# Two PSUM banks that change roles at the end of each group of heads

## The chip, the cores and the metric

The kernel runs on one core of one Trainium2 chip. The metric is the device time of one execution in microseconds (us); the time given for a kernel is the median of its runs.

## The reference, cut to what matters

Four layers are stacked on a residual stream `x` of 2048 tokens by 576 features: attention (A), linear attention (B), A, B. All the work that the change touches lies in the two A layers and in that part of the B layers that is done while A still runs.

```
def _A_ref(x, wq, wk, wv, wo):                      # 32 heads of 18, one shared k and v
    q = (x @ wq).reshape(B, S, H, Dh).transpose(0, 2, 1, 3)
    k, v = x @ wk, x @ wv
    scores = einsum("bhqd,bkd->bhqk", q, k) * Dh ** -0.5
    p = softmax(scores)
    return einsum("bhqk,bkd->bhqd", p, v).transpose(...).reshape(B, S, H * Dh) @ wo

x = x + _A_ref(_layernorm(x), A_wq, A_wk, A_wv, A_wo)
x = x + _B_ref(_layernorm(x), B_wqkv, B_w_phi, B_wo)   # feature maps, per-head state, read-out
x = x + _A_ref(...)
x = x + _B_ref(...)
```

## The kernel before

**Tiling of the attention.** The 2048 queries are four chunks of 512 (`CW`), the 32 heads eight groups of four (`NG`, `GH`). A layer thus has 32 pairs of chunk and group, the list `groups`; below, "group" means such a pair. For each group the program runs over the 16 key tiles `t` of 128 keys. For one key tile it makes the scores of four heads (four matmuls, line 451, into two tiles `sc` of two heads each), takes their exponentials on ScalarE (line 952, `pt<-sc`), and multiplies them into the sum (`add_values`, line 738: four matmuls of 32 rows, one for each head, into the tile `acc`). The sum over the 16 key tiles builds up in `acc`, one PSUM bank of 128 x 512 floats. In the trace each of the matmuls of line 738 has two records, so one key tile shows as x8; in the order of the program's instructions it shows as x4.

**PSUM.** There are eight banks. While `attend` runs, three tiles `sc` take six of them, `acc` one (pool `psa`, one buffer) and `ps` one (pool `psm`, one buffer). Through `ps` goes everything that is not attention.

**Units, bursts and the fill.** `attend` cuts the work of groups 1 to 31 into units of one key tile and two heads. It issues three units of scores (a burst), then sums, then three more units, and so on; the sums run behind the scores. After every second burst it calls `fill()`, which takes one step of other work from a queue called `bulk`: the folding of the feature weights (`fold_phi`, lines 290 to 321; first layer only), and then, for each finished chunk, its output projection and most of the B layer (`chunk_work`: projections at line 205, `update_state` at line 526). A step writes one tile `ps`, and a copy or an addition on VectorE reads it. A projection is 14 matmuls; its cost on the program's own scale is 1750, over `HEAVY`, and then the sum of that burst is put off: the next one takes three key tiles. Smaller steps are followed at once by the sum of one key tile. So TensorE's order repeats every six units: six score matmuls, a step of fill, its sums, six score matmuls, its sums. This is called a period below. `in_order` chains TensorE's instructions in the order in which they are written.

**The end of a group.** After the sixteenth key tile, `finish_group` copies `acc` to SBUF on VectorE (line 865, `osb<-acc`), and sends the denominators through DRAM and back (lines 867 to 883). The next group's sum goes to a new tile `acc` of the same pool. The pool has one buffer, so the first matmul of the next group waits until the copy at line 865 has ended. TensorE executes in order: score matmuls and fill behind the waiting matmul wait too. Where the group ends inside a burst, the first matmuls of the next group stand right behind the last ones of this group; where it ends with the burst, six score matmuls, and perhaps a step of fill, stand between them.

For what follows the 30 ends of groups that matter in a layer are numbered: boundary k lies between the sums of groups k and k + 1, with k from 1 to 30.

## Time and profile before

| | |
|---|---|
| time, median of 3 runs | 2824.49 us (2821.88 to 2828.26) |
| the profiled execution: its time, its span | 2827.11 us, 2825.3 us |
| attention of the first layer, `attend` | about 168 to 1243 us of the span |
| attention of the second layer | about 1560 to 2632 us |
| TensorE busy, over the span | 2658.9 us (94%) |
| ScalarE busy | 2189.0 us (77%) |
| VectorE busy | 1242.3 us (44%) |

The page of the profile adds up busy times over the span. A wait has a row of its own in the view of waits: who waited, for whom, the total, how often, and the longest. In the timeline every row gives the start, the length, the engine, the line, what is written and read, how many instructions were merged (x8), and in brackets how long the engine stood idle ahead of it and for what. "PE" is TensorE's matmuls, "PEld" its weight loads, "DVE" VectorE, "ACT" ScalarE, "SPq" the queue that issues the DMAs. The end of a matmul is modelled: matmuls overlap, so that the matmuls of one key tile start 0.11 us apart and each is shown with some 0.59 us.

### The profile page before, as it was taken

To read this page: it belongs to the slowest core of one execution; us is meant where nothing else is said; L and a number is where in the kernel's file an instruction comes from. 1 tells how busy PE (TensorE), PEld (TensorE's weight loads), DVE (VectorE), ACT (ScalarE), POOL (GpSimd) and SP (SyncE) were. 2 spreads that over 40 slices of the span, in tenths; PEclk is the share of its full clock that TensorE was granted. 3 is DMA by queue.
4 is the path that set the end of the run, shared out by engine and by line. 5 is a ranking of instruction groups with operands and counts; after the bars stand their busy time and mean duration, and the time that the engine had idled before them with its cause. 6 is when DMAs were issued, how large, how long until landed. Compare 5 with 4: busy or idle time off the path is not lost. (4 is left out here: it accounts for less than half of the span.)

```text
span 2825.3 us, 55543 instructions
## 1 busy us (share of the span) xinstructions
PE 2658.9 (94%) x22094; PEld 1458.3 (52%) x22094; DVE 1242.3 (44%) x2899; ACT 2189.0 (77%) x2644; POOL 86.0 (3%) x123
## 2 busy tenths in 40 slices
PE   6989999998999899998999888999989998999989
PEld 5733335443454345468986222355435453455788
DVE  6421224542355334558763301145424542454675
ACT  4579998898889888964345899989888888898521
POOL 1000000000000000004000000000000000000110
PEclk9999999999999999999999999999999999999999
DMA  5322233222222223234632311132123212321344
GB/s 184 103 67 62 67 97 92 61 48 57 71 81 54 58 58 96 52 80 120 186 123 89 87 37 34 43 94 60 42 65 99 57 39 68 91 62 43 103 119 139
DMA packets 355814, 224.97 MB, mean 80 GB/s; under 512 B 206874, under 2 KB 288986, under 8 KB 355546
## 3 DMA queue, kind: packets, MB, share of 16 engines
q1 hardware_dynamic: 355546, 221.31, 28.3%
q8 instruction: 178, 2.92, 0.4%
q14 instruction: 90, 0.74, 0.1%
HBM read 132.88 MB, written 67.03 MB: 71 GB/s over the span
## 5 line engine op out<-in xcount | busy, mean ns | idle before, releaser
L952 ACT ACTIVATE pt<-sc 128x1024 f32<-128x1024 f32 x1984 | 1874.5, 1031 | 216.3 <-PE sc L451 197.5
L738 PE MATMUL acc<-pt,vst 128*32 128x512 f32 x7936 | 966.6, 604 | 33.0 <-DVE osb L865 33.0
L451 PE MATMUL sc<-qst,kst 56*128 56x512 f32 x3840 | 696.3, 448 | 63.7 <-ACT pt L952 63.2
L451 PEld LDWEIGHTS sc<-qst,kst 56*128 56x128 f32 x3840 | 320.9, 185 | 620.8 <-ACT pt L952 556.0
L738 PEld LDWEIGHTS acc<-pt,vst 128*32 128x32 f32 x7936 | 209.5, 110 | 470.0 <-issue 401.0
L205 PE MATMUL ps<-wahi,xs 128*128 128x288 f32 x1035 | 226.5, 305 | 1.0 <-ACT xs L137 0.9
L205 PEld LDWEIGHTS ps<-wahi,xs 128*128 128x128 f32 x1035 | 170.0, 189 | 18.9 <-issue 12.7
L865 DVE COPY osb<-acc 128x512 f32<-128x512 f32 x62 | 42.6, 688 | 295.5 <-PE acc L738 266.2
L205 PE MATMUL ps<-walo,xs 128*128 128x288 f32 x575 | 169.3, 296 | 0.0
L262 DVE TENSOR_TENSOR xc<-xc,ps 128x288 f32<-128x288 f32 x77 | 34.5, 449 | 217.9 <-PE ps L205 217.9
L205 PE MATMUL ps<-wchi,on 128*128 128x288 f32 x549 | 121.7, 306 | 1.8 <-DMA on<-parts 1.8
L205 PE MATMUL ps<-wchi,xs 128*128 128x288 f32 x540 | 119.7, 307 | 1.7 <-ACT wchi L137 1.6
L205 PE MATMUL ps<-wbhi,xs 128*128 128x288 f32 x540 | 118.5, 305 | 0.0
L229 POOL TENSOR_TENSOR rstd<-var,neghalf 128x1 f32<-128x1 f32 (+1 forms) x56 | 33.1, 592 | 2534.5 <-DVE var L227 1755.1
L205 PEld LDWEIGHTS ps<-walo,xs 128*128 128x128 f32 x575 | 108.7, 189 | 0.0
L883 DVE TENSOR_TENSOR osb<-osb,parts 128x512 f32<-128x512 f32 x62 | 42.6, 688 | 139.7 <-DMA parts<-den_rows 139.7
L355 PE MATMUL ps<-xsc,wbhi 128*128 128x256 f32 x513 | 98.3, 287 | 5.8 <-DVE xsc L140 2.3
L205 PEld LDWEIGHTS ps<-wchi,on 128*128 128x128 f32 x549 | 90.2, 188 | 19.2 <-issue 16.6
L205 PEld LDWEIGHTS ps<-wchi,xs 128*128 128x128 f32 x540 | 88.4, 188 | 20.0 <-issue 17.5
L205 PEld LDWEIGHTS ps<-wbhi,xs 128*128 128x128 f32 x540 | 88.3, 188 | 17.5 <-issue 15.7
L137 ACT ACTIVATE xs<-ps 128x512 fp32r<-128x512 f32 x34 | 20.3, 596 | 93.3 <-PE ps L248 93.2
L205 PE MATMUL ps<-wclo,xs 128*128 128x288 f32 x300 | 89.0, 297 | 2.3 <-DVE wclo L140 2.3
(282 smaller groups left out, 2944.0 us busy)
## 6 DMA issues: line engine op xcount, KB each, us to landing
qst<-qd SPq DMA_DIRECT2D x360, 72.0 KB
pht<-phi SPq DMA_DIRECT2D x32, 540.0 KB
qd<-pcs SPq DMA_DIRECT2D x64, 256.0 KB
parts<-den_rows SPq DMA_DIRECT2D x62, 256.0 KB
wstage<-folded SPq DMA_DIRECT2D x50, 288.0 KB
on<-parts SPq DMA_DIRECT2D x192, 72.0 KB
phi<-pht SPq DMA_DIRECT2D x96, 144.0 KB
wstage<-in_A_wo_dram SPq DMA_DIRECT2D x32, 288.0 KB
```

The lines of the kernel that those rows point to most:

```text
L137: A.activation(dst_hi, src, AF.Copy)
L205: T.matmul(dst, xs[:, slot, :], w[half][:, k, c0 : c0 + HALF], start=(n == 0), stop=(n == last))
L229: G.tensor_tensor(rstd, var, neghalf[:, :n], op=ALU.pow)
L262: V.tensor_add(xr, xr, po)
L355: T.matmul(po, lhs, xsc[:, slot, :], start=(n == 0), stop=(n == LASTP))
L451: T.matmul(sc, kst[head_rows(h), t * P : (t + 1) * P], q[head_rows(h), h // 2, :], start=True, stop=True)
L738: T.matmul(acc[32 * j : 32 * j + 32, :], vst[:, t, :], pts[j], start=first, stop=last)
L865: V.tensor_copy(osb, acc[c, g])
L883: V.tensor_mul(osb, osb, den)
L952: A.activation(pt, sc, AF.Exp, scale=SCALE)
```

## The change

The banks `acc` and `ps` trade their roles. `homes` holds the two places; a new sum takes the first, and every tile of the fill takes the second (`Spare`). At the first sum of a group the list is reversed, except for group 1, whose place is the usual one. The last group of a layer has the usual place again, since 30 reversals lie between. A small function `bank` cuts a tile of the wanted shape out of a bank. The loop of bursts is written as two functions, `scores` and `sums`; the rest is the same work.

```diff
+            homes = [(psa, "acc"), (psm, "ps")]
+
+            class Spare:
+                def tile(self, shape, dtype, name):
+                    return bank(*homes[1], shape)
...
-                    bulk.append(after_chunk(c, on[c], psm, loads))
+                    bulk.append(after_chunk(c, on[c], Spare(), loads))
...
             def values(c, g, t, pt):
                 if t == 0:
-                    acc[c, g] = psa.tile([P, CW], F32, name="acc")
+                    if (c, g) != groups[1]:
+                        homes.reverse()
+                    acc[c, g] = bank(*homes[0], [P, CW])
...
-            bulk.append(extra(a1, psm, loads))
+            bulk.append(extra(a1, Spare(), loads))
...
-                    pt = a1.tile([P, 2, 512], F32, name="pt", bufs=9)
+                    pt = a1.tile([P, 2, 512], F32, name="pt", bufs=3 * BURST)
...
+            while at[0] < len(units):
+                sums(scores(BURST))
                 tick()
-                if not odd:
-                    tick()
-            for n, t, _ in units[2 * done :: 2]:
-                values(*groups[n], t, [pts.pop((n, t, hh)) for hh in range(2)])
                 tick()
+                ready = scores(BURST)
+                spent = fill()
                 in_order()
+                if spent < HEAVY:
+                    sums(ready)
+                tick()
...
+    def bank(pool, tag, shape):
+        t = pool.tile([P, CW], F32, name=tag)[: shape[0]]
+        if len(shape) == 2:
+            return t[:, : shape[1]]
+        return t[:, : shape[1] * shape[2]].rearrange("p (a b) -> p a b", b=shape[2])
```

The instructions of TensorE and of ScalarE stand in the same order as before; on TensorE only the bank that each writes is another. The places on which the prediction rests are these.

TensorE at boundary 8 of a layer (`wchi`, `wclo` are the output projection's weights, `on` the normalised sums), before:

```order
L205 MATMUL ps<-wclo_2485,on 128x288
L451 MATMUL sc<-qst,kst 128x512 x6
L738 MATMUL acc<-pt,vst 32x512 x12
L451 MATMUL sc<-qst,kst 128x512 x6
L205 MATMUL ps<-wchi,on 128x288
```

and now:

```order
L205 MATMUL acc<-wclo_2485,on 128x288
L451 MATMUL sc<-qst,kst 128x512 x6
L738 MATMUL ps<-pt,vst 32x512 x8
L738 MATMUL acc<-pt,vst 32x512 x4
L451 MATMUL sc<-qst,kst 128x512 x6
L205 MATMUL ps<-wchi,on 128x288
```

The twelve matmuls are two key tiles of the old group and one of the new. Before, all wrote one bank; now the third key tile writes the bank that the projection ahead of it used, and the projection behind it takes the bank that the copy of the old group reads.

TensorE at boundary 3 of the first layer, where a step of `fold_phi` (line 312) stands right ahead of the new group's first key tile, before:

```order
L738 MATMUL acc<-pt,vst 32x512 x8
L451 MATMUL sc<-qst,kst 128x512 x6
L312 MATMUL ps<-featq,xn 128x126 x4
L738 MATMUL acc<-pt,vst 32x512 x4
L451 MATMUL sc<-qst,kst 128x512 x6
```

and now:

```order
L738 MATMUL acc<-pt,vst 32x512 x8
L451 MATMUL sc<-qst,kst 128x512 x6
L312 MATMUL ps<-featq,xn 128x126 x4
L738 MATMUL ps<-pt,vst 32x512 x4
L451 MATMUL sc<-qst,kst 128x512 x6
```

The step of fill and the first sum of the new group now write the same bank, one right behind the other.

VectorE's queue is ordered by a scheduler, and some instructions trade places with their neighbours. The copy of a group's sum moves behind other work at boundary 7 of the first layer (a pair of weight instructions) and at boundaries 15 and 23 of both; at boundary 15 it stood so (`wstage`, `wchi`, `wclo` are the output projection's weights on their way in):

```order
L576 STREAM_TRANSPOSE pht<-featq 128x1152
L865 COPY osb<-acc 128x512
L139 CAST wchi<-wstage 128x576
L140 TENSOR_TENSOR wclo_7440<-wstage,wchi 128x576
L873 RECIPROCAL rd<-rd 128x16
```

and now stands so:

```order
L576 STREAM_TRANSPOSE pht<-featq 128x1152
L140 TENSOR_TENSOR wclo_7440<-wstage,wchi 128x576
L139 CAST wchi<-wstage 128x576
L140 TENSOR_TENSOR wclo_7440<-wstage,wchi 128x576
L870 COPY osb<-acc 128x512
L878 RECIPROCAL rd<-rd 128x16
```

The splitting of two pieces of weights has moved ahead of the copy. At boundary 10, of which the prediction also speaks, VectorE's order is the same before and now.

## The prediction

> **What bounds the kernel now.** The page comes first, for the bound and for the group that the change touches.

> ```profile
> span 2825.3 us, 55543 instructions
> PE 2658.9 (94%) x22094; PEld 1458.3 (52%) x22094; DVE 1242.3 (44%) x2899; ACT 2189.0 (77%) x2644; POOL 86.0 (3%) x123
> ...
> L738 PE MATMUL acc<-pt,vst 128*32 128x512 f32 x7936 | 966.6, 604 | 33.0 <-DVE osb L865 33.0
> ...
> L865 DVE COPY osb<-acc 128x512 f32<-128x512 f32 x62 | 42.6, 688 | 295.5 <-PE acc L738 266.2
> ```

> TensorE is busy for 94% of the span. Ahead of the sums (line 738) it idles 33.0 us, all of it for the copy of a group's sum, which takes 0.69 us. The view of waits for TensorE says how often.

> ```profile
> PE sc L451 <- ACT pt L952: 67.9, 200, 1.8
> PE acc L738 <- DVE osb L865: 33.0, 34, 2.4
> ...
> PE ps L205 <- DVE wclo L140: 2.3, 5, 0.9
> ...
> PE ps L205 <- DMA on<-parts: 1.8, 2, 0.9
> ```

> There are 34 waits, in 62 copies. The boundaries without one have six score matmuls or a fill between the old group's last sum and the new group's first. Whether a wait costs time is a question for the stage, since 67.9 us of waits for ScalarE show that TensorE is not the bound everywhere. So I read the timeline in a stretch with projections (boundary 26, second layer):

> ```profile
> 2454.55 2.78 PE L738 MATMUL acc<-pt,vst 128*32 128x512 f32 x24
> ...
> 2461.20 1.92 PE L738 MATMUL acc<-pt,vst 128*32 128x512 f32 x16
> ...
> 2463.20 0.69 DVE L865 COPY osb<-acc 128x512 f32<-128x512 f32 x1 [2.41 <-PE acc L738]
> ...
> 2463.94 1.07 PE L738 MATMUL acc<-pt,vst 128*32 128x512 f32 x8 [0.81 <-DVE osb L865]
> ...
> 2468.88 2.78 PE L738 MATMUL acc<-pt,vst 128*32 128x512 f32 x24
> ```

> From the sums of one period to the next it is 2461.20 - 2454.55 = 6.65 us; the period with the boundary takes 2468.88 - 2461.20 = 7.68. It is longer by 1.03, not by 0.81: the ends of matmuls are modelled, and without a wait a key tile starts while the one ahead still counts as running. (Three key tiles take 2.78, one 1.07, so they start 0.86 apart; the third would have started at 2461.20 + 1.72 = 2462.92, and started 1.02 later.) I take **0.2 us on top of the wait that the profile shows**.

> In the second layer's first stretch there is no fill, and ScalarE should be the bound:

> ```profile
> 1621.48 1.92 PE L738 MATMUL acc<-pt,vst 128*32 128x512 f32 x16
> ...
> 1627.28 1.06 PE L738 MATMUL acc<-pt,vst 128*32 128x512 f32 x8
> 1629.16 1.07 PE L738 MATMUL acc<-pt,vst 128*32 128x512 f32 x8 [0.81 <-DVE osb L865]
> ...
> 1634.10 1.92 PE L738 MATMUL acc<-pt,vst 128*32 128x512 f32 x16
> ...
> 1630.76 2.85 ACT L952 ACTIVATE pt<-sc 128x1024 f32<-128x1024 f32 x3 [1.22 <-PE sc L451]
> ```

> A period there is 1627.28 - 1621.48 = 5.80, with the boundary 1634.10 - 1627.28 = 6.82: again 1.02 more. ScalarE ran dry for 1.22 us, because the next scores stand behind the waiting sum. So the wait is paid in both kinds of stretch.

> **The change part by part.** *The 34 waits go.* The new group writes another bank. Two of the 34 (boundary 28 of each layer) have score matmuls between, so nothing overlapped there and the 0.2 is not added: 33.0 + 32 x 0.2 = 39.4 us.

> *Two of them cost more than the wait.* At boundary 25 of each layer the copy stands behind a transposition in VectorE's queue:

> ```profile
> 749.68 1.06 PE L738 MATMUL acc<-pt,vst 128*32 128x512 f32 x8 [1.50 <-DVE osb L865]
> ...
> 1036.61 0.65 DVE L865 COPY osb<-acc 128x512 f32<-128x512 f32 x1
> 1037.32 3.44 PE L738 MATMUL acc<-pt,vst 128*32 128x512 f32 x16 [2.37 <-DVE osb L865]
> 1041.71 0.40 PE L205 MATMUL ps<-wchi,on 128*128 128x288 f32 x1
> ...
> 2427.44 3.28 PE L738 MATMUL acc<-pt,vst 128*32 128x512 f32 x16 [2.35 <-DVE osb L865]
> ...
> 1037.30:1040.70 3.40, 3.38 (x18) 0.60 (x18) 0.00 (x0) 0.00 (x0) 0.00 (x0) 0.54 0.40 69
> 749.70:750.70 1.00, 1.00 (x10) 0.16 (x10) 0.00 (x0) 0.00 (x0) 0.00 (x0) 1.00 0.00 0
> ```

> After waits of 2.37 and 2.35 us two key tiles take 3.44 and 3.28 instead of 1.92, and the granted clock in that stretch (the column ahead of the DMA share) is 0.54. After the next longest wait, 1.50 us at boundary 17, it is 1.00. Without the wait the slow matmuls go too: 1.52 + 1.36 = 2.9 us more. [...]

> *One wait comes back.* At boundary 10 of each layer VectorE splits weights behind the copy:

> ```profile
> 498.82 0.69 DVE L865 COPY osb<-acc 128x512 f32<-128x512 f32 x1 [1.56 <-PE acc L738]
> ...
> 503.71 0.46 DVE L139 CAST wchi<-wstage 128x576 fp32r<-128x576 f32 x1 [1.87 <-DMA wstage<-folded]
> ...
> 504.20 0.76 DVE L140 TENSOR_TENSOR wclo<-wstage,wchi 128x576 fp32r<-128x576 f32 x1
> ...
> 505.02 0.40 PE L205 MATMUL ps<-wclo,xs 128*128 128x288 f32 x1 [0.39 <-DVE wclo L140]
> ```

> This chain starts when the old group's last sum ends, which the change doesn't move, and goes over a DMA; TensorE already waits for its end at 505.02. It would come 1.0 earlier and wait 1.0 longer: **-2.0 us** in two layers.

> *Two new waits.* At boundaries 3 and 6 of the first layer a step of fill writes the bank right ahead of the new group:

> ```profile
> 268.81 1.06 PE L738 MATMUL acc<-pt,vst 128*32 128x512 f32 x8
> 268.92 0.68 DVE L314 COPY featk<-ps 128x504 f32<-128x504 f32 x1 [1.30 <-PE ps L312]
> 363.28 1.06 PE L738 MATMUL acc<-pt,vst 128*32 128x512 f32 x8
> 363.39 0.28 DVE L296 COPY xn<-ps 72x128 f32<-72x128 f32 x1 [0.40 <-PE ps L295]
> ```

> The sum must wait for the end of the copy, from 268.81 to 269.60 and from 363.28 to 363.67, and 0.05 for the signal: 0.85 + 0.45 = **-1.3 us**. Behind them wait the next scores, and ScalarE for these.

> *No cost I expect at the other boundaries,* for two covers. First, where a projection stands ahead, six score matmuls stand between it and the new sum. The tightest kind (14 boundaries, k = 9, 12 and the like):

> ```profile
> 570.91 0.29 PE L205 MATMUL ps<-walo,xs 128*128 128x288 f32 x1
> ...
> 571.24 0.46 DVE L482 COPY featk<-ps 128x288 f32<-128x288 f32 x1 [2.25 <-PE ps L205]
> ...
> 572.10 1.49 PE L738 MATMUL acc<-pt,vst 128*32 128x512 f32 x11
> ```

> The bank is read out at 571.70, 0.40 before it is wanted, and VectorE had idled 2.25 before. Were that cover gone by half a microsecond, 14 x 0.5 = 7 us. Second, the next projection now writes the bank of the old sum, behind the copy. At boundary 25 it would start 4.1 earlier (2.37 + 0.2 + 1.52) than 1041.71, at 1037.6; the copy ends at 1037.26. That cover is thin, but only the boundaries with a late copy have so little. The weights that VectorE now splits ahead of the copy at boundaries 7, 15 and 23 delay a copy that nobody on TensorE waits for any more; I cost that at nothing. Instructions are neither added nor removed on TensorE and ScalarE.

> Sum: 39.4 + 2.9 - 2.0 - 1.3 = **39.0 us** less.

> **The rivals.** *Half comes back.* Scores, fill and sums are one order on TensorE, so what arrives 1.0 us earlier may meet a chain of VectorE and DMA, as at boundary 10: the finish of a group, the flipped tokens, the weights. For it speaks that this is seen once in each layer; against it, that the projections (line 205) wait for nothing else for more than the 2.3 and 1.8 us in the list above. With half of the 39.0 gone, 2824.5 - 19.5 = 2805.

> *No gain.* If TensorE only trades one wait for the next, everything comes back at the following scores, which wait for ScalarE (67.9 us of such waits): 2824. Against it stands ScalarE's 1.22 of idle time above, which the boundary made. [...]

> *Slower.* The 14 boundaries that have no wait now would get one, if VectorE read the projection's bank late: behind a feature chain or a transposition. From 2.4 us on, the slow clock adds 1.5, so that each costs 4: 14 x 4 = 56, less 39, gives 2824.5 + 17 = 2842. The point of balance is 39 / 14 = 2.8 us for each. Against it: the read-out above starts right at the projection's end, on an idle VectorE.

> **How the numbers follow.** The profiled execution took 2827.1 us with a span of 2825.3; the median of the runs is 2824.5, inside their spread of 2821.9 to 2828.3. I take the saving from the median: 2824.5 - 39.0 = 2785.5, rounded to 2786. Chances: the sum as worked out 75%, half comes back 17%, no gain 4%, slower 4%. If nothing came back (39.4 + 2.9 = 42.3) and the run were as fast as the lowest shown (2.6 below), 2779.6; if the 14 tight places lost 0.5 each (7 us) and the run were as slow as the highest (3.8 above), 2796; a little of the second case takes it to 2800. So 2779 to 2800. 0.2% (5.6 us) is about what a measurement of this kernel can tell from no change: faster 92%, same 4%, slower 4%.

> **What would show it.** In the changed profile the row of line 738 waiting for the copy of `osb` should be gone, or down to about 1.3 us with two waits, on the copies of `fold_phi`. Periods with a boundary should take 6.65 and 5.80 us. The period with boundary 10 should not get shorter, and wait longer for `wclo`. No sum should run at a slow clock behind boundary 25. The prediction is wrong if line 738 waits for other VectorE instructions in many places, if projections wait for the copy of `osb`, or if ScalarE's busy share does not rise.

## The result, and the profile after

| | before | after |
|---|---|---|
| time, median | 2827.2 us (2821.9 to 2832.3, 6 runs) | 2775.1 us (2774.5 to 2778.9, 6 runs) |
| span of the profiled execution | 2825.3 us | 2773.3 us |

The ratio is 0.9817, with a 95% interval of 0.9803 to 0.9831. The kernel got 52 us faster; the prediction said 39 and had 2779 as its lower end. The direction and the mechanism came out as forecast, but 13 us came from somewhere else. The page of the changed kernel first (busy times, then the two groups of line 738, one for each bank):

```profile
span 2773.3 us, 55536 instructions
PE 2646.9 (95%) x22094; PEld 1459.3 (53%) x22094; DVE 1243.3 (45%) x2899; ACT 2190.3 (79%) x2644; POOL 86.1 (3%) x123
...
L738 PE MATMUL acc<-pt,vst 128*32 128x512 f32 x4096 | 498.4, 604 | 0.5 <-DVE xn L296 0.4
L738 PE MATMUL ps<-pt,vst 128*32 128x512 f32 x3840 | 463.2, 598 | 0.8 <-DVE featk L314 0.8
```

Of the 33.0 us that line 738 idled, 1.3 are left, and nothing in them waits for `osb`. The same 22094 matmuls run, and both TensorE and ScalarE fill more of a shorter span. TensorE's waits:

```profile
PE sc L451 <- ACT pt L960: 59.3, 190, 0.5
...
PE acc L205 <- DMA on<-parts: 2.8, 2, 1.5
...
PE ps L205 <- DVE wchi L139: 1.8, 2, 0.9
...
PE ps L738 <- DVE featk L314: 0.8, 1, 0.8
...
PE acc L738 <- DVE xn L296: 0.4, 1, 0.4
```

The last two rows are the two new waits of the forecast, 0.8 and 0.4 us. The first row is the surprise: waits for ScalarE's exponentials were 67.9 us with a longest of 1.8, and are 59.3 with a longest of 0.5. The row for `on<-parts` has grown from 1.8 to 2.8 us, and the one for `wchi` is new. Boundary 26 of the second layer in the timeline:

```profile
2406.28 2.78 PE L738 MATMUL ps<-pt,vst 128*32 128x512 f32 x24
...
2412.94 1.92 PE L738 MATMUL ps<-pt,vst 128*32 128x512 f32 x16
2414.68 1.04 PE L738 MATMUL acc<-pt,vst 128*32 128x512 f32 x8
2414.93 0.69 DVE L870 COPY osb<-ps 128x512 f32<-128x512 f32 x1 [2.42 <-PE ps L738]
...
2419.59 2.78 PE L738 MATMUL acc<-pt,vst 128*32 128x512 f32 x24
```

The new group starts in the other bank while VectorE still copies the old one, and the two periods around the boundary take 2412.94 - 2406.28 = 6.66 and 2419.59 - 2412.94 = 6.65 us. To see where the 52 us came from, the 330 periods of attention (165 in each layer, cut at the first score matmul of each period) were matched between the two profiled executions and their differences added up by place:

| place | periods | forecast, us | measured, us |
|---|---|---|---|
| boundaries with a wait, without 10 and 25 | 30 | -32.3 | -32.3 |
| boundary 25, with its slow matmuls | 2 | -8.0 | -8.2 |
| boundary 10, its own period | 2 | 0 | -0.2 |
| the period behind boundary 10 | 2 | 0 | **+3.2** |
| boundaries 3 and 6 of the first layer | 2 | +1.3 | +1.3 |
| at the finish of groups 14 and 22 | 8 | 0 | **-13.8** |
| the wait for `on<-parts` (boundary 16) | 2 | 0 | +1.1 |
| all others | 282 | 0 | -1.8 |
| sum | 330 | -39.0 | -50.7 |

The sum of the rows is 50.7 of the 52.0 us by which the spans differ; the other 1.3 lies outside these periods. The largest row that the forecast doesn't have is made at four places, two periods each, two places in a layer: while groups 14 and 22 are being finished (their sums ended some 15 us earlier) and a chunk's last token tile ends in `update_state`. There are no waits for `osb` there. The timeline of the first of them, in the kernel before:

```profile
657.89 0.69 DVE L883 TENSOR_TENSOR osb<-osb,parts 128x512 f32<-128x512 f32 x1 [2.30 <-DMA parts<-den_rows]
658.50 0.45 DVE L487 TENSOR_TENSOR featq<-featq,fmax 128x288 f32<-128x288 f32 x1
...
658.99 0.68 ACT L489 ACTIVATE featq<-featq 128x576 f32<-128x576 f32 x1 [2.86 <-DVE featq L487]
...
660.64 0.51 PE L451 MATMUL sc<-qst,kst 56*128 56x512 f32 x2 [1.73 <-ACT pt L952]
...
663.19 3.06 PE L738 MATMUL acc<-pt,vst 128*32 128x512 f32 x16
```

and in the changed kernel:

```profile
651.34 0.45 DVE L487 TENSOR_TENSOR featq<-featq,fmax 128x288 f32<-128x288 f32 x1
...
651.83 0.69 ACT L489 ACTIVATE featq<-featq 128x576 f32<-128x576 f32 x1 [0.64 <-DVE featq L487]
...
655.70 0.69 DVE L888 TENSOR_TENSOR osb<-osb,parts 128x512 f32<-128x512 f32 x1 [2.35 <-DMA parts<-den_rows]
655.73 1.92 PE L738 MATMUL acc<-pt,vst 128*32 128x512 f32 x16
```

Read from top to bottom, the first block is one chain. The multiplication of `osb` by the reciprocals (line 883, now 888) waits 2.30 us for a DMA that brings them back from DRAM. Behind it in VectorE's queue stands a subtraction on `featq` (line 487) that needs nothing from that DMA. ScalarE's exponential of `featq` (line 489) waits for the subtraction, 2.86 us, and behind it wait the exponentials of attention; TensorE waits for these (1.73 us), and its next two key tiles take 3.06 us in place of 1.92: from 662.11 to 665.52 us the granted clock, the share of TensorE's full clock that it is given, is 0.50. In the second block the subtraction stands ahead. The multiplication still waits 2.35 us for the same DMA, but nobody on the path waits for it. So the change has two parts: the banks, and an order of VectorE's queue that its scheduler made anew (some DMAs in SyncE's queue have traded places too; ScalarE's order in attention is the same). The reading that this order, not the banks, brought the 13.8 us is tested next.

### The profile page after: what moved, and what is told of

Same layout as the page of the kernel before. It is cut to its first block, busy times and chain, and to the rows that moved or that the text cites. A ratio compares the mean times of both kernels' runs of the same rounds, so it can differ in the third digit from the quotient of the medians.

```text
span 2773.3 us, 55536 instructions
## 1 busy us (share of the span) xinstructions
PE 2646.9 (95%) x22094; PEld 1459.3 (53%) x22094; DVE 1243.3 (45%) x2899; ACT 2190.3 (79%) x2644; POOL 86.1 (3%) x123
## 5 line engine op out<-in xcount | busy, mean ns | idle before, releaser
L451 PE MATMUL sc<-qst,kst 56*128 56x512 f32 x3840 | 694.6, 448 | 54.7 <-ACT pt L960 54.4
L451 PEld LDWEIGHTS sc<-qst,kst 56*128 56x128 f32 x3840 | 319.2, 184 | 609.8 <-ACT pt L960 567.1
L738 PE MATMUL acc<-pt,vst 128*32 128x512 f32 x4096 | 498.4, 604 | 0.5 <-DVE xn L296 0.4
L738 PE MATMUL ps<-pt,vst 128*32 128x512 f32 x3840 | 463.2, 598 | 0.8 <-DVE featk L314 0.8
L738 PEld LDWEIGHTS acc<-pt,vst 128*32 128x32 f32 x4096 | 110.3, 110 | 225.6 <-issue 219.5
L738 PEld LDWEIGHTS ps<-pt,vst 128*32 128x32 f32 x3840 | 101.4, 109 | 202.0 <-issue 197.6
L205 PE MATMUL ps<-wahi,xs 128*128 128x288 f32 x801 | 173.9, 303 | 1.0 <-ACT xs L137 0.9
L205 PEld LDWEIGHTS ps<-wahi,xs 128*128 128x128 f32 x801 | 130.9, 188 | 10.1 <-issue 6.8
L205 PE MATMUL ps<-walo,xs 128*128 128x288 f32 x445 | 130.7, 296 | 0.0
L205 PE MATMUL ps<-wchi,xs 128*128 128x288 f32 x414 | 91.8, 306 | 2.2 <-DVE wchi L139 1.8
L205 PE MATMUL ps<-wchi,on 128*128 128x288 f32 x405 | 89.2, 304 | 0.0
L355 PEld LDWEIGHTS ps<-xsc,wbhi 128*128 128x128 f32 x513 | 82.1, 192 | 6.9 <-DVE xsc L140 2.6
L205 PEld LDWEIGHTS ps<-walo,xs 128*128 128x128 f32 x445 | 83.7, 188 | 0.0
L355 PE MATMUL ps<-xsc,wblo 128*128 128x256 f32 x285 | 79.0, 284 | 0.0
```

The source lines that it names most:

```text
L205: T.matmul(dst, xs[:, slot, :], w[half][:, k, c0 : c0 + HALF], start=(n == 0), stop=(n == last))
L355: T.matmul(po, lhs, xsc[:, slot, :], start=(n == 0), stop=(n == LASTP))
L451: T.matmul(sc, kst[head_rows(h), t * P : (t + 1) * P], q[head_rows(h), h // 2, :], start=True, stop=True)
L738: T.matmul(acc[32 * j : 32 * j + 32, :], vst[:, t, :], pts[j], start=first, stop=last)
```

## The experiments

Times are set against the runs of the kernel before on the same chip, which gave 2826.0, 2824.9 and 2826.5 us in the three groups of runs.

**The order at two boundaries, without the exchange.** The code cuts below show the lines that matter, `...` stands for lines left out. The kernel before, with the multiplication at boundaries 14 and 22 put behind the subtraction by a dependence that only sets the order:

```diff
...
                 V.tensor_mul(osb, osb, den)
+                if (c, g) in (groups[14], groups[22]):
+                    mul = [i for i in traced(nc) if i.engine == mybir.EngineType.DVE][-1]
+                    tc.add_manual_dep(mul, behind.name, NOSYNC, reason="order")
```

(`behind` is the last VectorE instruction written ahead of the multiplication, the subtraction.)

> The kernel before, banks not exchanged; at boundaries 14 and 22 of each layer VectorE's multiplication of a group's sum by its denominators (line 883, it waits for a DMA) stands behind the subtraction of line 487 instead of ahead of it. Theory A (the gain beyond the forecast is VectorE's order: ScalarE's exponential of line 489 waited for line 487, and with it the attention's exponentials): those four places return to about 6.2 and 5.6 us a period, and the span falls by 13.8 us against the kernel before, a ratio of 0.995. Theory B (the exchange of the banks itself, or the time at which the DMA lands): no change, 1.000. The 34 waits of line 738 stay in both.

Measured: 2810.0 us (2807.9 to 2811.3), ratio 0.9943 (0.9926 to 0.9959). The eight periods got 13.9 us shorter, against 13.8 in the change. The timeline of this kernel at the first place:

```profile
656.23 0.68 ACT L489 ACTIVATE featq<-featq 128x576 f32<-128x576 f32 x1 [0.54 <-DVE featq L487]
...
657.57 0.69 DVE L884 TENSOR_TENSOR osb<-osb,parts 128x512 f32<-128x512 f32 x1 [1.37 <-DMA parts<-den_rows]
...
660.14 1.92 PE L738 MATMUL acc<-pt,vst 128*32 128x512 f32 x16
```

The stall and the slow key tiles are gone while all 34 waits for `osb` are still there. Trading two VectorE instructions at four places makes these 13.8 us. (The scheduler moved a few neighbours with them: a piece of weights with the DMA that fetches it, and the next copy of `osb`.) Another 3.0 us of this profiled execution are at boundary 25, where its periods take 9.2 us instead of 10.9 and 10.6, without the slow clock.

**The old order in the changed kernel, at boundary 22.**

```diff
...
                 V.tensor_mul(osb, osb, den)
+                if (c, g) == groups[22]:
+                    mul = [i for i in traced(nc) if i.engine == mybir.EngineType.DVE][-1]
+                    tc.add_manual_dep(behind, mul.name, NOSYNC, reason="order")
```

> The changed kernel, banks exchanged; at boundary 22 of each layer line 888 (the multiplication) stands ahead of line 487, as it did before the change. Theory A: ScalarE's exponential waits about 2.9 us there again, and the span grows by what the two places cost before: 3.9 us in the first layer and 2.3 in the second, 2773.3 to about 2779.5 (ratio to the kernel before 0.984). Theory B: no change against the changed kernel.

Measured: 2789.6 us (2786.1 to 2793.0), ratio 0.9865 (0.9848 to 0.9881). The stall comes back, and the time is 10 us above the 2779.5 expected: the four periods at boundary 22 take 13.4 us more than in the changed kernel, where the kernel before had lost 6.2. Its timeline at boundary 22 of the first layer:

```profile
935.10 0.69 DVE L889 TENSOR_TENSOR osb<-osb,parts 128x512 f32<-128x512 f32 x1 [3.15 <-DMA parts<-den_rows]
...
936.19 0.68 ACT L489 ACTIVATE featq<-featq 128x576 f32<-128x576 f32 x1 [4.38 <-DVE featq L487]
...
937.84 0.66 PE L451 MATMUL sc<-qst,kst 56*128 56x512 f32 x2 [3.24 <-ACT pt L964]
```

**The same at boundaries 14 and 22.** The condition above reads `(c, g) in (groups[14], groups[22])`.

> The changed kernel with VectorE's old order at both boundaries 14 and 22 (the multiplication of osb by the reciprocals, which waits for its DMA, ahead of the subtraction of featq): the exchange of banks without the trade of places in VectorE's queue. If exchange and order add up: the four places, of 13.8 us in all, come back, and the time is 2775 + 14 = 2789, which is the exchange as predicted, 38 us less than before. If they do not add: at boundary 22 alone the old order cost 13.4 us in the changed kernel against 6.2 us in the kernel before, since TensorE and the features reach the place earlier and the denominators' way over DRAM takes as long as ever; with boundary 14 the same, 2775 + 27 = 2802, and a part of the 34 waits comes back as waits of ScalarE for featq.

Measured: 2794.6 us (2791.3 to 2797.2), ratio 0.9891 (0.9874 to 0.9907). That is 19.5 above the changed kernel: more than what the places were worth, less than the 27 of the second case. In the trace the reason is another pair of instructions: in the new order the reciprocal of the denominators stands behind work on the features and the weights, and goes out later. The timeline of the kernel before, from the copy at boundary 14 on:

```profile
641.33 0.69 DVE L865 COPY osb<-acc 128x512 f32<-128x512 f32 x1 [2.43 <-PE acc L738]
...
650.76 0.24 DVE L873 RECIPROCAL rd<-rd 128x16 f32<-128x16 f32 x1
```

and of this kernel, at the same boundary of its second layer:

```profile
2011.80 0.69 DVE L870 COPY osb<-ps 128x512 f32<-128x512 f32 x1 [2.42 <-PE ps L738]
...
2022.48 0.25 DVE L878 RECIPROCAL rd<-rd 128x16 f32<-128x16 f32 x1
...
2030.07 0.69 DVE L889 TENSOR_TENSOR osb<-osb,parts 128x512 f32<-128x512 f32 x1 [2.31 <-DMA parts<-den_rows]
```

The reciprocal comes 9.43 us behind the copy in the one and 10.68 in the other, the multiplication 657.89 - 641.33 = 16.56 and 18.27 (the kernel before has 9.44 and 16.59 in its second layer). So this run isn't the exchange by itself. The scheduler had moved more than one instruction, and the two moves belong together: the late reciprocal costs nothing only because the subtraction no longer stands behind its answer.

**The exchange alone, and the order alone.** Two kernels settle it. In the first, the changed kernel has the instructions of VectorE, ScalarE and SyncE in attention chained in the order of the kernel before; in the second, the kernel before has them in the order of the changed kernel. `ranks` is a list of positions for each layer and engine, `mine` the engine's instructions in attention as they were written.

```diff
+            begun = len(traced(nc))
             attend(layer, st, a1o, extra, after_chunk, chunks)
...
+                for a, b in zip(ranks, ranks[1:]):
+                    tc.add_manual_dep(mine[b], mine[a].name, NOSYNC, reason="order")
```

> The exchange of banks alone: the changed kernel, with the instructions of VectorE, ScalarE and SyncE in attention chained in the order that they have in the kernel before, so that every engine's queue reads as before and only the banks differ. The prediction's sum was made for this kernel: 39.0 us less than before, 2786 to 2787. Theory (the chains through VectorE and DRAM at the places after the last token tile of chunks 1 and 2 start at the copy of the old group and don't move, while TensorE arrives 1.0 us earlier, as at boundary 10): the four places keep their stalls and lose 1.0 us each, and the two places after boundary 10 lose 1.6 us each to the slow clock that the changed kernel shows there; 39.0 - 4.0 - 3.2 = 31.8, so 2793 to 2795. Rival (the run with only the multiplication moved back, 2795, was bad because the reciprocals of the denominators had also moved back in the new order): 2790 or better.

Measured: 2792.7 us (2790.4 to 2796.6), ratio 0.9882 (0.9866 to 0.9899): 33.8 us less than before. The number is 0.3 us below the expected 2793 to 2795, and the working held only in part. The period behind boundary 10 cost 3.3 us in the two layers, as expected. The four places lost 3.3 us, not through 1.0 each. The timeline at the first of them (the lists stand ahead in the file, so the lines are others: 1099 is the copy, 1117 the multiplication, 718 the exponential of `featq`, 680 the scores, 967 the sums), and behind it the view of two stretches, at these places in the second layer:

```profile
637.99 0.69 DVE L1099 COPY osb<-ps 128x512 f32<-128x512 f32 x1 [2.42 <-PE ps L967]
...
653.49 0.69 DVE L1117 TENSOR_TENSOR osb<-osb,parts 128x512 f32<-128x512 f32 x1 [2.26 <-DMA parts<-den_rows]
...
654.59 0.68 ACT L718 ACTIVATE featq<-featq 128x576 f32<-128x576 f32 x1 [2.83 <-DVE featq L716]
...
656.24 0.50 PE L680 MATMUL sc<-qst,kst 56*128 56x512 f32 x2 [1.69 <-ACT pt L1189]
...
2029.53:2036.35 6.82, 6.51 (x26) 1.99 (x26) 3.42 (x6) 4.32 (x6) 0.00 (x0) 0.50 0.30 62
2312.83:2319.66 6.83, 6.43 (x26) 2.00 (x26) 3.92 (x7) 4.33 (x6) 0.00 (x0) 0.50 0.23 49
```

From copy to multiplication it is 15.50 us here, 1.06 less than before: the reciprocal stands behind a step of features, so the chain moves along with TensorE, and the stall stays at 1.69. The 3.3 us are slow matmuls, all in the second layer: the last two rows show the granted clock (the third number from the end) at 0.50 for 6.83 us at both places, where the kernel before had 3.41 us of it at one and none at the other.

The second kernel:

> The order alone: the kernel before, banks not exchanged, with the instructions of VectorE, ScalarE and SyncE in attention chained in the order that they have in the changed kernel. Theory: the four places give their 14 us, as in the run that moved only the multiplication (2810); against it, at boundaries 15 and 23 of both layers the copy of a group's sum now stands behind a pair of weight instructions of 0.46 and 0.76 us, and here TensorE still waits for that copy: 2 x (1.1 + 1.2) = 4.6 us. So about 2815. If nobody waits for these copies either: 2810. If exchange and order simply add up to the 52 us of the change, this kernel and the one with the banks alone must together be 52 us less than twice the kernel before; the theory says less (some 32 + 10), the rest being the delay of the copies, which only the exchange takes off the path, and the stalls, which only the order takes off.

Measured: 2811.3 us (2810.3 to 2813.1), ratio 0.9948 (0.9931 to 0.9965): 15.3 us less than before, of which 13.7 are at the four places. The delay of the copies at boundaries 15 and 23 that I expected isn't there: those periods differ by 0.12 us or less. The weights that moved ahead of the copy use time in which VectorE was idle: ahead of the copy at boundary 15 it still has 6.53 us of it. Exchange and order alone give 33.8 + 15.3 = 49.1 of the 52.1 us, which agree within their intervals. By the periods two terms keep the parts from adding up, and they go against each other: the 3.3 us of slow clock at the four places, which the exchange adds and the order takes away, and 3.0 us of slow clock at boundary 25, which are gone in both kernels and so are counted twice.

**The wait at boundary 25.** The changed kernel, with no reversal at boundaries 24 and 25, so that the new group there has the old group's bank again (at 24 two bursts of scores and a projection stand between, at 25 nothing):

```diff
-                    if (c, g) != groups[1]:
+                    if (c, g) not in (groups[1], groups[25], groups[26]):
```

> The changed kernel, but the banks keep their roles at boundaries 24 and 25 of each layer (two, so that the last group ends in the usual bank). Boundary 24 has no wait in either kernel. At 25 the wait of 2.4 us returns. If a wait of that length also slows the clock: 4.2 and 3.9 us, 8.1 together, span about 2781, and key tiles at 1.5 us more there. If only the wait is paid: 2 x 2.57 = 5.1, span about 2778.5.

Measured: 2783.6 us (2780.3 to 2787.2), ratio 0.9844 (0.9827 to 0.9861). The same wait costs 4.2 us in the first layer and 2.6 in the second, by the periods. The timeline in the two layers:

```profile
1020.97 3.08 PE L738 MATMUL ps<-pt,vst 128*32 128x512 f32 x16 [2.35 <-DVE osb L870]
...
2392.12 1.93 PE L738 MATMUL ps<-pt,vst 128*32 128x512 f32 x16 [2.36 <-DVE osb L870]
```

So the wait costs 2.6, which is the 2.36 and 0.2 of the prediction, and the slow clock 1.6 more in one of two cases. The median went up by 8.5 us. The profiled execution, the slowest of the four, has a span 12.2 longer: 6.8 are these two periods, 1.65 a slow stretch behind boundary 16, and 3.1 lie outside attention.

**The weights first at boundary 10.** The changed kernel, with the two pairs of `wchi` and `wclo` that have landed put ahead of the copy of `osb` at this boundary (`meet` puts the copy behind the second of them):

```diff
                 V.tensor_copy(osb, acc[c, g])
+                if (c, g) == groups[10]:
+                    held["copy"] = latest(mybir.EngineType.DVE)
+                    meet()
...
```

> The changed kernel; at boundary 10 of each layer VectorE splits the two pieces of weights that have landed (lines 139, 140) ahead of the copy of the group's sum. If the chain from that copy to the last piece is what holds the projection there: the chain starts about 1.2 us earlier, the waits for wchi and wclo (0.94 and 0.40) shrink to a few tenths, and if the slow clock of the next period hangs on these waits, its 1.6 us go too: 5 to 7 us less in two layers, span about 2767. If the slow clock there has another cause: about 2.5 us less, span about 2771. If the chain is held by the DMA alone: no change.

Measured: 2768.5 us (2767.5 to 2772.1), ratio 0.9793 (0.9777 to 0.9809). The timeline of the changed kernel behind boundary 10 shows why it was worth that much:

```profile
500.94 0.40 PE L205 MATMUL ps<-wchi,xs 128*128 128x288 f32 x1 [0.94 <-DVE wchi L139]
501.73 0.40 PE L205 MATMUL ps<-wclo,xs 128*128 128x288 f32 x1 [0.40 <-DVE wclo L140]
503.06 4.32 PE L738 MATMUL acc<-pt,vst 128*32 128x512 f32 x24
```

and so does the view of two stretches there (busy times of TensorE, its weight loads, VectorE, ScalarE and GpSimd, then the granted clock, the DMA share and GB/s):

```profile
499.38:502.79 3.41, 2.08 (x13) 1.24 (x11) 1.80 (x4) 1.45 (x3) 0.00 (x0) 1.00 0.63 183
502.79:506.20 3.41, 3.41 (x20) 0.79 (x20) 1.68 (x5) 3.30 (x4) 0.00 (x0) 0.50 0.38 129
```

Behind two waits of 0.94 and 0.40 us (before: one of 0.39) the granted clock falls to 0.50 for 3.41 us, and three key tiles take 4.32 us instead of 2.78. With the weights first, both waits and the slow stretch are gone (in the first layer the three key tiles at 501.40 us take 2.78 us) and the two periods take 6.6 to 6.9 us: 3.4 and 3.2 us in the two layers.

**The packing copies first.** The changed kernel, with the DMAs `on<-parts` of group 15 put ahead of the fetch of the queries of group 18 in SyncE's queue (`order_queue` puts the fetch behind them):

```diff
+            if n == 18:
+                queued["fetch"] = [i for i in traced(nc)[before:] if i.engine == mybir.EngineType.SP]
+                order_queue()
...
```

> The changed kernel, with one move in SyncE's queue: the copies that pack the normalised sums of the second chunk's last group (on<-parts) stand ahead of the fetch of the queries three groups on, not behind it. Theory (the order of the queue made the wait): the two waits of projections for on<-parts, 1.3 and 1.5 us, go, and the periods at that place come down from 8.58 and 8.78 us to about 7; about 3 us less than the changed kernel's 2775, so 2772. Rival (the copies are late by the DMAs ahead of them, the denominators' way through DRAM, not by the queue): the waits stay at about 1 us and more, as before the change, and the time stays at 2775. Third: the queries fetched later make the scores of their group late; a wait for qst shows, and the time is 2775 or above.

Measured: 2773.2 us (2770.7 to 2775.2), ratio 0.9813 (0.9797 to 0.9830). The two waits are gone and their periods take 7.0 us instead of 8.6 and 8.8, but the time is 51.8 us below the kernel before where the changed kernel's is 52.1: the 3.3 us that the two periods gave don't show in the time of this kernel. The runs can't decide it, since the interval of the ratio, 0.9797 to 0.9830, is 9 us wide. In the profiled execution the periods of attention together are 2.3 us shorter than in the changed kernel, and the time outside them is 1.2 longer; in the eleven profiled executions that time lies anywhere between 674.4 and 681.2 us.

**All three, with no exchange at boundaries 3 and 6.** There six score matmuls separate the old sum from the new one, so the old bank costs nothing, while the exchange put a step of fill on the new sum's bank.

> The changed kernel with three repairs: the two pieces of weights ahead of the copy at boundary 10 (as in the run with the weights first), the packing copies ahead of the fetch of the queries, and no exchange at boundaries 3 and 6, where a step of fill stands right ahead of the new sum and six score matmuls stand between the old sum and it. If they add: 6.6 us (boundary 10, both layers), 3 us (packing copies) and 1.3 us (the two waits for featk and xn) less than 2775, so 2764. If they meet each other (a period that gets shorter moves the next wait forward, or a clock drop comes back elsewhere): no better than the run with the weights first, 2768. If not exchanging at 3 and 6 brings the waits for the copy of osb back there: two waits of about 1 us of line 738 for osb, and 2765 to 2766.

Measured: 2763.5 us (2760.4 to 2766.7), ratio 0.9785 (0.9768 to 0.9801): faster than both kernels, 61.4 us below the kernel before. The three gains add up: against the changed kernel the periods at and behind boundary 10 are 6.7 us shorter, those with the packing copies 3.3, those at boundaries 3 and 6 1.3, and all of attention 11.0.

```profile
span 2758.6 us, 55540 instructions
...
L740 PE MATMUL acc<-pt,vst 128*32 128x512 f32 x4352 | 527.5, 601 | 0.1
L740 PE MATMUL ps<-pt,vst 128*32 128x512 f32 x3584 | 431.2, 598 | 0.0
```

The sums (line 740 here) wait for next to nothing any more, and the mean granted clock of this execution is 0.992, where the kernel before and the changed kernel have 0.989.

## Why the prediction was wrong, point by point

**The 34 waits** were right in place and size. Thirty periods gave 32.3 us where 33.0 and 32 times 0.2, without boundaries 10 and 25, give 32.3; the 0.2 us that the profile doesn't show as waiting was real.

**Boundary 25** was right in its sum (8.2 us), with luck in its second part. The wait alone costs 2.6 us. The slow clock came behind 3 of the 8 waits of 2.35 to 2.37 us that the runs have at this boundary: both in the kernel before, one of two in the run above, and in neither kernel that had only the order changed, where the period took 9.2 us instead of 10.9 and 10.6. The 2.9 us were what this one execution had lost, not what the wait costs each time.

**Boundary 10** was right in the chain. It didn't move: from the copy to the end of the wait for `wclo` it is 505.02 - 498.82 = 6.20 us before and 501.73 - 495.67 = 6.06 after, and TensorE waits 0.95 longer. The term of -2.0 was mis-sized by 3.2 us: the longer wait cost the clock in the period behind it, in both layers. I had given the slow clock only to waits of 2.4 us.

**The two new waits** came as forecast, 0.83 and 0.45 us in their periods. **The other boundaries** have no new wait, and the thin cover at boundary 25 held: the projection there starts 0.24 us behind the end of the copy, and the period takes 6.66 us.

```profile
2380.54 1.90 PE L738 MATMUL ps<-pt,vst 128*32 128x512 f32 x16
...
2382.38 0.65 DVE L870 COPY osb<-acc 128x512 f32<-128x512 f32 x1
...
2383.27 0.40 PE L205 MATMUL acc<-wchi,on 128*128 128x288 f32 x1
```

**The step that failed** is the one on VectorE's new order. The prediction asked of the moved instructions only whether they delay the copy of `osb`, found that nobody waits for it any more, and put the reordering down at nothing. For the copy that was right; the order alone shows no cost at boundaries 15 and 23. But the same reordering took the subtraction of `featq` out from behind an instruction that waits for a DMA, and this freed ScalarE's queue, 13.8 us at four places. The rows to see it by were in the kernel before: a VectorE instruction with 2.30 us of idle time for a DMA, and an exponential with 2.86 us behind it. The view of ScalarE's waits had it too. Before:

```profile
ACT featq L489 <- DVE featq L487: 24.6, 13, 2.9
```

and after:

```profile
ACT featq L489 <- DVE featq L487: 15.1, 13, 2.6
```

In the kernel before, the subtraction on VectorE stood behind the multiplication and its wait of 2.30 us, and the exponentials of attention on ScalarE stood behind that of `featq` and its wait of 2.86 us; neither needs the result of what it stood behind.

**The rivals.** Half coming back was seen at boundary 10 alone, a late bank at none of the 14 tight boundaries. The exchange by itself, for which the sum of 39.0 was made, gave 33.8 us, so no gain is out too, and its 2792.7 lies inside the range of 2779 to 2800. By its periods, the places that the sum names gave 39.0; 3.3 us were lost behind boundary 10 and 3.3 at the four places, and 1.3 us of small gains elsewhere are not explained. It was the order, which the prediction had put at nothing, that took the changed kernel out of the range.

## What to carry to other kernels

Where a scheduler orders a queue, a change to one resource reorders instructions that have nothing to do with it. Go through every pair that traded places and ask what each of them waits for: here an instruction that waited 2.30 us for a DMA on VectorE held up the subtraction behind it, and the price was found two engines further on, as waits of 2.86 us on ScalarE and 1.73 us on TensorE. To price a change of two parts, run each part alone with the other's order held fixed.

## What the runs showed of the hardware

```profile
1034.17:1037.58 3.41, 1.04 (x12) 0.16 (x8) 2.27 (x6) 2.19 (x3) 0.54 (x1) 1.00 0.01 2
1037.58:1040.99 3.41, 3.41 (x18) 0.73 (x12) 0.00 (x0) 0.00 (x0) 0.00 (x0) 0.50 0.49 85
```

The wait from 1034.96 to 1037.32 lies within the first of them, and the second is slow. In the second layer the wait ends at 2427.44, and 1.71 of its 2.35 us lie ahead of the slow stretch that begins at 2426.80. The length of the wait alone didn't decide: in the run that brought it back, two key tiles took 3.08 us behind 2.35 us of it and 1.93 behind 2.36. That it matters where the wait falls among these stretches is an estimate from these waits; no run took it apart.

TensorE's busy time ahead of the slow stretches was counted too. The attention of the kernel before and of the changed kernel, cut into stretches of 3.4133 us counted from a slow one, without 20 us at either end of a layer, gives 1183 stretches at the full clock. Two of them, with TensorE busy for 1.04 and 1.21 us, are followed by a slow one, and none of the 1172 with 2.19 or more is; of the nine in between, from 1.54 to 2.17 us, five are. Two of these five hold the waits behind boundary 10 of the changed kernel: TensorE is busy for 2.08 us beside waits of 0.94 and 0.40 us and for 2.17 beside 0.84 and 0.40, and 3.41 us at 0.50 follow. What decides among the nine stays open.
